# Turning the first 512 rows of x: four row blocks on TensorE, where two were turned on TensorE and two by a transposing load

## The chip, the cores and the metric

The kernel runs on one core of a Trainium2 chip. The metric is the device time of one execution in microseconds (us), as the median of several runs. Engines are named as the profile names them: PE is TensorE's matmul stream and PEld its weight loads, DVE is VectorE, ACT is ScalarE, POOL is GpSimd, SP is the SyncE queue that issues most loads and stores.

## The reference: what is computed

Two independent attention problems, A and B, have the same shape, and their outputs are joined along the last axis. Each has 2048 rows of x with 1024 columns, 32 heads of 32, and a sliding window of 256 keys. In short form:

```python
qkv = (x @ wqkv).reshape(B, S, 3, H, Dh)          # S = 2048, H = 32, Dh = 32
scores = q @ k.T * Dh ** -0.5                     # per head
mask = (i - j >= 0) & (i - j < 256)               # query i, key j
p = softmax(where(mask, scores, -1e9))
out = (p @ v).reshape(B, S, D) @ wo               # D = 1024
result = concatenate([A, B], axis=-1)
```

Inputs and output are bf16.

## The kernel before, in words

**Tiles.** x is held transposed in four quarters of 512 rows per problem, `xT[(pi, k)]`: 128 partitions, eight column tiles (`ct`), 512 rows. A row block is 128 rows, so a quarter has four of them (`QB` = 4). Heads are taken in groups of four (`g`, eight per problem, 16 in all). A group has a weight tile `wqk[g]` with a q half and a k half (`which` 0 and 1), and every two groups share a tile `wv[m]`.

**Chains and sessions.** The TensorE work is of two sorts. Projections are cut into *chains*: eight matmuls of 512 columns, or sixteen of 256, which fill one PSUM bank and end with a cast out of it. There are chains for q and k of a group and a quarter (`qk_steps`, L198), for v of two row blocks (`v_steps`, L216) and for the output (`out_steps`, L262). Their bank comes from `ps_proj`, which has two. A *session* (L438) is the score matmuls of four block pairs (L451), one exp over them on ACT (L459), and the masks on POOL. There are 180 sessions. The PV matmuls with the row sums (L513) follow three sessions after the last scores that they need, then the norm on VectorE.

**What sets the order.** The program is written out in order by a planner. Each chain has an `early` and a `late` session. In each session, `emit` places filler steps from the chain with the smallest `late` that may start, until a budget is spent. The budget is `level(now) - fixed[now]` (L426): the work that must be done by, or is available by, each later session, averaged, and never more than `NS_MOST` = 3300 ns. `fixed` holds 440 ns for a session's scores and 55 ns for each PV step. `forced` (L418) ends what is due. `evacuate` (L188) chooses ScalarE or VectorE for a cast by a model of their clocks (`_Clock`, L60). `whole` says if a chain's matmuls take all 128 output columns at once (L172) or in four strips of 32 (L176); strips are used in sessions in which a PV is due.

**The start, which the change touches.** The kernel begins with dummy matmuls on a zeroed tile, `keep_warm`. Row blocks 0 and 1 of problem A's x are loaded as they lie (L548) into `xrow`, slices of a tile `rows`. `flip(a)` (L575) turns one block: eight 128x128 transposes into one PSUM bank (L578), then a copy of one half of that bank by ACT (L582) and of the other by DVE (L583) into `xT[(0, 0)]`. Row blocks 2 and 3 come by a transposing load, `load_x(0, 0, 2, 2)` (L133, issued on SP). Quarters 1 to 3 come by transposing loads of 512 rows behind it on the same queue, with the weights of group 1 and the second v tile between them. `first(lo, hi)` (L585) does the columns from `lo` to `hi` of q and k of group 0 and quarter 0; q's bank is taken from `ps_acc`, k's from `ps_proj`. `emit(0, chains[0].size)` places one whole v chain; it stands twice, once ahead of the last `first` and once behind it. Then the loop over sessions begins.

Of the kernel before, what the change touches and what calls it, by code (L numbers as in the profile page):

```python
# [8 lines left out]
BF16 = mybir.dt.bfloat16  # L9
F32 = mybir.dt.float32  # L10
# [8 lines left out]
P = 128  # L19
# [7 lines left out]
QB = 4  # L27
SLOTS = 4
# [50 lines left out]
def _fast_path(ctx, tc, cfg, problems, outs, consts, certify):  # L79
    nc = tc.nc  # L80
# [8 lines left out]
    clock = _Clock()  # L89
# [27 lines left out]
    ps_st = ctx.enter_context(tc.tile_pool(name="ps_st", bufs=1, space=PSUM))  # L117
    ps_acc = ctx.enter_context(tc.tile_pool(name="ps_acc", bufs=2, space=PSUM))
    ps_proj = ctx.enter_context(tc.tile_pool(name="ps_proj", bufs=2, space=PSUM))
# [6 lines left out]
    blank = top[:].bitcast(BF16)  # L126

    def new_x(pi, k):
        xT[(pi, k)] = xpool.tile([P, CT, 512], BF16, name="xT")

    def load_x(pi, k, a=0, n=QB, c0=0, c1=CT):
        lo, hi = a * P, (a + n) * P
        nc.sync.dma_start_transpose(  # L133
            out=xT[(pi, k)][:, c0:c1, lo:hi],
            in_=problems[pi][0][k * 512 + lo:k * 512 + hi, c0 * P:c1 * P])
# [7 lines left out]
    def load_wqk(g, which, queue, lo=0, hi=CT):  # L143
        pi, t = divmod(g, T)
        queue.dma_start(out=wqk[g][:, lo:hi, which, :],  # L145
                        in_=wsrc(pi)[:, lo:hi, which, t * P:(t + 1) * P])

    def new_wv(m):
        wv[m] = wvp.tile([P, CT, VG * P], BF16, name="wv")

    def load_wv(m, lo, hi, queue):
        pi, mm = divmod(m, T // VG)
        w_ = VG * P
        queue.dma_start(out=wv[m][:, lo:hi, :],  # L154
                        in_=wsrc(pi)[:, lo:hi, 2, mm * w_:(mm + 1) * w_])
# [9 lines left out]
    def qk_tiles(g):  # L165
        if g not in qks:
            qks[g] = (qkp.tile([P, S], BF16, name="qT"), qkp.tile([P, S], BF16, name="kT"))
        return qks[g]

    def by_columns(out, lo, hi, lhsT, rhs, start, stop):  # L170
        if whole[0]:
            nc.tensor.matmul(out[:, lo:hi], lhsT=lhsT, rhs=rhs, start=start, stop=stop,  # L172
                             skip_group_check=True)
            return
        for c in range(0, P, 32):
            nc.tensor.matmul(out[c:c + 32, lo:hi], lhsT=lhsT[:, c:c + 32], rhs=rhs, start=start,  # L176
                             stop=stop, tile_position=(0, c), skip_group_check=True)
# [4 lines left out]
    def add_or(dst):  # L182
        def f():
            nc.vector.tensor_tensor(out=top[:], in0=top[:], in1=dst.bitcast(I32),
                                    op=ALU.bitwise_or)
        side.append((COST["or"], f, False))

    def evacuate(out, in_, engines=("act", "dve")):  # L188
        if clock.evacuate(engines) == "act":
            nc.scalar.copy(out=out, in_=in_)  # L190
        else:
            nc.vector.tensor_copy(out=out, in_=in_)

    def new_pp():
        clock.chain()
        return ps_proj.tile([P, 512], F32, name="pp")

    def qk_steps(g, which, k, lo=0, hi=512, st_=None, last=True):  # L198
        pi = g // T
        st_ = {} if st_ is None else st_  # L200
        steps = []
        for ct in range(CT):
            def f(ct=ct):
                if "pp" not in st_:
                    st_["pp"] = new_pp()
                by_columns(st_["pp"], lo, hi, wqk[g][:, ct, which, :], xT[(pi, k)][:, ct, lo:hi],
                           ct == 0, ct == CT - 1)
                clock.pe += NS_MM * (hi - lo) / 512.0
                if ct == CT - 1 and last:
                    dst = qk_tiles(g)[which][:, k * 512:(k + 1) * 512]  # L210
                    evacuate(dst, st_["pp"][:])
                    add_or(dst)
            steps.append((NS_MM * (hi - lo) / 512.0, f))
        return steps
# [138 lines left out]
    chains = []  # L353
# [39 lines left out]
    def start_chain(now):  # L393
        for n, c in enumerate(chains):
            if c.early <= now:
                current.extend(chains.pop(n).steps)
                return True
        return False

    def run_side():  # L400
        cost, f, last = side.pop(0)
        f()
        clock.dve = max(clock.dve, clock.pe) + cost
        if last:
            clock.norms.append(clock.dve)

    def emit(now, budget):
        done = 0.0
        while (current or chains) and done < budget - 0.5 * (current[0][0] if current else NS_MM):
            if not current and not start_chain(now):  # L410
                break
            ns, f = current.pop(0)
            f()
            done += ns
            if side and (clock.dve < clock.pe + 100.0 or len(side) > 8):
                run_side()
# [124 lines left out]
    rows = opool.tile([P, T, 512], BF16, name="oT")  # L541
    new_x(0, 0)
    new_wqk(0)
    new_wv(0)
    xrow = [rows[:, 2 * a:2 * a + 2, :].rearrange("p t n -> p (t n)") for a in range(2)]
    load_wqk(0, 0, nc.scalar)
    for a in range(2):
        nc.sync.dma_start(out=xrow[a], in_=problems[0][0][a * P:(a + 1) * P, :])  # L548
        if a == 0:
            load_wqk(0, 1, nc.sync)  # L550
    load_wv(0, 0, CT, nc.sync)
    load_x(0, 0, 2, 2)
    new_x(0, 1)
    load_x(0, 1)
    new_wqk(1)
# [6 lines left out]
            new_wv(1)  # L562
            load_wv(1, 0, CT, nc.sync)

    warm = ps_st.tile([P, 4, SLOTS, P], F32, name="st")[:, 1].rearrange("p a q -> p (a q)")

    def keep_warm(n):
        for _ in range(n):
            nc.tensor.matmul(warm, lhsT=blank[:, 0:P], rhs=blank[:, 0:512], start=True, stop=True)

    keep_warm(6)
    flips = [ps_acc.tile([P, 512], F32, name="acc")[:]]
    held = [{"pp": ps_acc.tile([P, 512], F32, name="acc")[:]}, {}]

    def flip(a):  # L575
        f = flips[0].bitcast(BF16).rearrange("p (ct q) -> p ct q", q=P)
        for ct in range(CT):
            nc.tensor.transpose(out=f[:, ct, :], in_=xrow[a][:, ct * P:(ct + 1) * P],  # L578
                                identity=ident[:])
        dst = xT[(0, 0)][:, :, a * P:(a + 1) * P]  # L580
        half = CT // 2
        nc.scalar.copy(out=dst[:, :half, :], in_=f[:, :half, :])  # L582
        nc.vector.tensor_copy(out=dst[:, half:, :], in_=f[:, half:, :])  # L583

    def first(lo, hi):  # L585
        for which in range(2):
            for _, f in qk_steps(0, which, 0, lo, hi, held[which], last=hi == 512):
                f()

    flip(0)  # L590
    keep_warm(3)
    first(0, P)
    flip(1)
    keep_warm(3)
    first(P, 2 * P)
    emit(0, chains[0].size)
    first(2 * P, 4 * P)
    clock.banks = clock.banks[-2:]
    emit(0, chains[0].size)

    sealed = first_use(G - 1, NQ - 1, 0)
    for now in range(END):
# [3 lines left out]
        while due and due[0][0] <= now:  # L606
            _, pg, pk = due.pop(0)
# [14 lines left out]
    while due:  # L622
        _, pg, pk = due.pop(0)
# [132 lines left out]
def kernel(  # L756
# [48 lines left out]
    with tc.manual_schedule():  # L805
        with ExitStack() as fctx:
            _fast_path(fctx, tc, cfg, problems, outs, consts, [reduce_bits, decide])
# [40 lines left out]
```

## Time and profile before

| | us |
|---|---|
| median of 3 runs | 614.89 (614.78 to 615.02) |
| time of the profiled execution | 614.78 |
| its span in the trace | 613.0 |
| PE busy in the span | 594.8 (97%) |
| ACT busy | 453.7 (74%) |
| DVE busy | 446.8 (73%) |
| POOL busy | 328.0 (54%) |
| mean granted TensorE clock | 0.998 |

The span is the time between the first and the last instruction of the program in the trace; the time of the execution holds 1.8 us more. A busy share is an average over the whole span and tells little of a stage: the change lies in the first 20 us, and is to be read from the timelines of that stretch. In lines of a timeline the first number is the start in us from the span's beginning, the second the length; brackets hold the idle time ahead of the instruction and what ended it. "L172 PE MATMUL pp<-xT,wqk" is a matmul that writes tile pp from xT and wqk, recorded at line 172 of the kernel. Ends of matmuls are modelled, so that neighbouring pieces of PE can overlap.

### The profile page before, as it was taken

What the parts mean: (1) busy time and instruction counts of PE and PEld (TensorE: products, weight loads), DVE (VectorE), ACT (ScalarE), POOL (GpSimd) and SP (SyncE); (2) the same over time, 40 slices, a digit from 0 to 9 for tenths busy, and PEclk for the clock granted to TensorE, in tenths of its full rate; (3) what the DMA queues carried; (4) which work ended last, traced back from release to release, by engine and by line L of the source; (5) the groups of instructions that cost most, each with busy time, mean ns of one, the idle gap of its engine ahead of it and who ended that gap; (6) DMA issues with size and microseconds to landing.
All of it is one profiled execution on the core that took longest, in us unless ns stands there. A gap on an engine that the chain in (4) does not pass through costs nothing.

```text
span 613.0 us, 28647 instructions
## 1 busy us (share of the span) xinstructions
PE 594.8 (97%) x12725; PEld 344.5 (56%) x12777; DVE 446.8 (73%) x1169; ACT 453.7 (74%) x402; POOL 328.0 (54%) x630
## 2 busy tenths in 40 slices
PE   8899999999999999999999999999999999999996
PEld 6455466656655756554555756655445765445443
DVE  1477969887888788769688888877878687779200
ACT  2777888888888878887778777787877777776332
POOL 0465666666666666556565565555555555554000
PEclk9999999999999999999999999999999999999999
DMA  9924110111015601453111100112020030113222
GB/s 209 204 71 106 38 37 4 37 37 40 3 36 89 116 11 31 77 99 80 36 39 37 38 4 3 37 37 81 3 70 30 12 98 19 64 55 113 72 77 65
DMA packets 88594, 35.47 MB, mean 58 GB/s; under 512 B 67600, under 2 KB 88208, under 8 KB 88464
## 3 DMA queue, kind: packets, MB, share of 16 engines
q1 hardware_dynamic: 87424, 33.31, 22.7%
q8 instruction: 102, 1.67, 1.1%
q10 hardware_dynamic: 1040, 0.26, 0.2%
q14 instruction: 28, 0.23, 0.1%
HBM read 17.30 MB, written 8.39 MB: 42 GB/s over the span
## 4 chain that ended last, share of the span: by engine, by line
PE 91%; ACT 3%; issue 2%; DMA 1%; SPq 1%; DVE 0%; ACTq 0%; DVEq 0%
PE pp L176 42%; PE pp L172 26%; PE acc L513 13%; PE st L451 10%; ACT pt L459 2%; DMA xT<-in_A_x_dram 1%; SPq L133 1%; ACT kT L190 0%; ACT vt L190 0%; SPq L548 0%; ACT osb L190 0%; ACT qT L190 0%; DVE rinv L524 0%; SPq L154 0%; SPq L145 0%
## 5 line engine op out<-in xcount | busy, mean ns | idle before, releaser
L459 ACT ACTIVATE pt<-st 128x2048 bf16<-128x2048 f32 x180 | 338.0, 1878 | 87.7 <-PE st L451 67.3
L471 POOL TENSOR_SCALAR_AFFINE_SELECT pt<-pt 128x512 bf16<-128x512 bf16 x224 | 155.3, 693 | 145.5 <-ACT pt L459 144.3
L467 POOL TENSOR_SCALAR_AFFINE_SELECT pt<-pt 128x512 bf16<-128x512 bf16 x256 | 180.0, 705 | 88.3 <-ACT pt L459 88.3
L524 DVE RECIPROCAL rinv<-acc 128x128 f32<-128x128 f32 x128 | 122.1, 954 | 66.7 <-PE acc L513 65.4
L176 PE MATMUL pp<-xT,wqk 128*32 128x512 bf16 x2696 | 162.8, 379 | 0.2
L481 DVE TENSOR_TENSOR both<-pt 128x512 bf16<-128x512 bf16 x224 | 132.5, 631 | 0.0
L176 PEld LDWEIGHTS <-wqk 128*32 128x32 bf16 x2696 | 69.3, 97 | 54.5 <-issue 1.2
L172 PE MATMUL pp<-xT,wqk 128*128 128x512 bf16 (+2 forms) x319 | 75.9, 368 | 6.2 <-issue 3.0
L176 PE MATMUL pp<-wv,xT 128*32 128x256 bf16 x2376 | 74.0, 273 | 0.0
L451 PE MATMUL st<-qT,kT 32*128 32x384 bf16 (+2 forms) x1488 | 71.7, 269 | 0.0
L176 PEld LDWEIGHTS <-xT 128*32 128x32 bf16 x2376 | 62.3, 97 | 5.5
L529 DVE STREAM_SHUFFLE wide<-rinv 128x128 f32<-128x128 f32 x256 | 64.5, 297 | 0.0
L513 PE MATMUL acc<-pt,vt 128*32 128x128 bf16 (+1 forms) x2160 | 63.3, 239 | 0.0
L172 PE MATMUL pp<-wo_sb,oT 128*128 128x512 bf16 (+1 forms) x270 | 59.7, 373 | 1.7 <-issue 1.0
L190 ACT CAST osb<-pp 128x512 bf16<-128x512 f32 (+1 forms) x53 | 30.6, 577 | 39.1 <-PE pp L172 23.1
L451 PEld LDWEIGHTS <-kT 32*128 32x128 bf16 x1488 | 22.3, 92 | 64.3 <-issue 63.4
L531 DVE TENSOR_TENSOR oT<-acc,wide 128x256 bf16<-128x256 f32 x128 | 54.4, 425 | 4.4
L172 PEld LDWEIGHTS <-wqk 128*128 128x128 bf16 x382 | 34.4, 98 | 40.7 <-issue 9.0
L176 PE MATMUL pp<-wo_sb,oT 128*32 128x512 bf16 x948 | 55.4, 379 | 0.7 <-DVE unsafe_i L802 0.7
L172 PE MATMUL pp<-wv,xT 128*128 128x256 bf16 x430 | 53.2, 273 | 2.0 <-ACT kT L190 0.8
L513 PEld LDWEIGHTS <-vt 128*32 128x32 bf16 x2160 | 35.9, 96 | 26.3 <-issue 24.1
L172 PEld LDWEIGHTS <-xT 128*128 128x128 bf16 x430 | 40.6, 98 | 12.8 <-issue 6.0
(45 smaller groups left out, 382.2 us busy)
## 6 DMA issues: line engine op xcount, KB each, us to landing
out_dram<-osb SPq DMA_DIRECT2D x63, 128.0 KB, 1.8
wqk<-in_B_wqkv_dram SPq DMA_DIRECT2D x32, 128.0 KB, 2.7
wqk<-in_A_wqkv_dram SPq DMA_DIRECT2D x24, 128.0 KB, 2.8
wo_sb<-in_A_wo_dram SPq DMA_DIRECT2D x16, 128.0 KB, 2.2
wv<-in_B_wqkv_dram SPq DMA_DIRECT2D x16, 128.0 KB, 2.9
wo_sb<-in_B_wo_dram SPq DMA_DIRECT2D x16, 128.0 KB, 2.4
wv<-in_A_wqkv_dram SPq DMA_DIRECT2D x2, 512.0 KB, 5.7
wv<-in_A_wqkv_dram SPq DMA_DIRECT2D x8, 128.0 KB, 2.3
```

The lines of the kernel that those rows point to most:

```text
L172: nc.tensor.matmul(out[:, lo:hi], lhsT=lhsT, rhs=rhs, start=start, stop=stop, skip_group_check=True)
L176: nc.tensor.matmul(out[c:c + 32, lo:hi], lhsT=lhsT[:, c:c + 32], rhs=rhs, start=start, stop=stop, tile_position=(0, c), skip_group_check=True)
L190: nc.scalar.copy(out=out, in_=in_)
L451: nc.tensor.matmul(st[:, r, a:b, :], lhsT=kT[32 * r:32 * r + 32, j * P:(j + 1) * P], rhs=qT[32 * r:32 * r + 32, q * P:(q + b - a) * P], st ...
L459: nc.scalar.activation(out=pt[:, :, :n, :].rearrange("p r a q -> p r (a q)"), in_=st[:, :, :n, :].rearrange("p r a q -> p r (a q)"), func= ...
L467: nc.gpsimd.affine_select(out=blk, in_=blk, pattern=[[0, 4], [1, P]], compare_op=ALU.is_ge, fill=0.0, base=0, channel_multiplier=-1)
L471: nc.gpsimd.affine_select(out=blk, in_=blk, pattern=[[0, 4], [-1, P]], compare_op=ALU.is_gt, fill=0.0, base=0, channel_multiplier=1)
L481: nc.vector.tensor_tensor(out=both[:, :, h, :], in0=pts[s0][:, :, a0, :], in1=pts[s1][:, :, a1, :], op=ALU.add)
L513: nc.tensor.matmul(acc[32 * r:32 * r + 32, o:o + w_], lhsT=lhsT, rhs=src[:, r, :, :], start=(x == 0), stop=(x == len(moves) - 1), tile_pos ...
L524: nc.vector.reciprocal(out=rinv[:], in_=acc[:, 2 * P:3 * P])
L529: nc.vector.stream_shuffle(out=wide[:, h * P:(h + 1) * P], in_=rinv[:], mask=[16 * h] * 32)
L531: nc.vector.tensor_tensor(out=oTs[(pi, k)][:, t, (p % 2) * 256:(p % 2 + 1) * 256], in0=acc[:, 0:256], in1=wide[:], op=ALU.mult)
```

## The change

All four row blocks of the first quarter are loaded as they lie and turned with `flip`, and the transposing load of the last two goes. The two added loads stand on SP ahead of the load of `wv[0]`; row block 1 now stands ahead of the k half of `wqk[0]`. The banks change: the warm tile comes from `ps_proj`; flips 0, 1 and 3 use tiles of `ps_acc` and flip 2 one bank of the score tile; q and k of group 0 take both their banks from `ps_proj`. `first(which, lo)` now does 256 columns of one of q and k. The order becomes flip 0, flip 1, q of rows 0 to 255, flips 2 and 3, k of rows 0 to 255, q and k of rows 256 to 511. One v chain is placed ahead of the first session, where two were. The warm matmuls after flip 0 become four. The planner's functions and constants are the same in both.

```diff
-    xrow = [rows[:, 2 * a:2 * a + 2, :].rearrange("p t n -> p (t n)") for a in range(2)]
+    xrow = [rows[:, 2 * a:2 * a + 2, :].rearrange("p t n -> p (t n)") for a in range(QB)]
     load_wqk(0, 0, nc.scalar)
-    for a in range(2):
+    for a in range(QB):
         nc.sync.dma_start(out=xrow[a], in_=problems[0][0][a * P:(a + 1) * P, :])
-        if a == 0:
+        if a == 1:
             load_wqk(0, 1, nc.sync)
     load_wv(0, 0, CT, nc.sync)
-    load_x(0, 0, 2, 2)
     new_x(0, 1)
     load_x(0, 1)
...
-    warm = ps_st.tile([P, 4, SLOTS, P], F32, name="st")[:, 1].rearrange("p a q -> p (a q)")
+    warm = ps_proj.tile([P, 512], F32, name="pp")
...
     keep_warm(6)
-    flips = [ps_acc.tile([P, 512], F32, name="acc")[:]]
-    held = [{"pp": ps_acc.tile([P, 512], F32, name="acc")[:]}, {}]
+    flips = [ps_acc.tile([P, 512], F32, name="acc") for _ in range(2)]
+    flips = [f[:] for f in flips]
+    flips.append(ps_st.tile([P, 4, SLOTS, P], F32, name="st")[:, 0].rearrange("p a q -> p (a q)"))
+    flips.append(None)
+    held = [{}, {}]
 
     def flip(a):
-        f = flips[0].bitcast(BF16).rearrange("p (ct q) -> p ct q", q=P)
+        if a == 3:
+            flips[a] = ps_acc.tile([P, 512], F32, name="acc")[:]
+        f = flips[a].bitcast(BF16).rearrange("p (ct q) -> p ct q", q=P)
...
-    def first(lo, hi):
-        for which in range(2):
-            for _, f in qk_steps(0, which, 0, lo, hi, held[which], last=hi == 512):
-                f()
+    def first(which, lo):
+        for _, f in qk_steps(0, which, 0, lo, lo + 256, held[which], last=lo > 0):
+            f()
 
     flip(0)
-    keep_warm(3)
-    first(0, P)
+    keep_warm(4)
     flip(1)
     keep_warm(3)
-    first(P, 2 * P)
-    emit(0, chains[0].size)
-    first(2 * P, 4 * P)
-    clock.banks = clock.banks[-2:]
+    first(0, 0)
+    flip(2)
+    flip(3)
+    first(1, 0)
+    first(0, 256)
+    first(1, 256)
     emit(0, chains[0].size)
```

More of the change, by code (lines that the diff above doesn't have):

```diff
@@ L563, in _fast_path @@
             load_wv(1, 0, CT, nc.sync)
-    warm = ps_st.tile([P, 4, SLOTS, P], F32, name="st")[:, 1].rearrange("p a q -> p (a q)")
+    warm = ps_proj.tile([P, 512], F32, name="pp")
     def keep_warm(n):
         for _ in range(n):
-            nc.tensor.matmul(warm, lhsT=blank[:, 0:P], rhs=blank[:, 0:512], start=True, stop=True)
+            nc.tensor.matmul(warm[:], lhsT=blank[:, 0:P], rhs=blank[:, 0:512], start=True, stop=True)
     keep_warm(6)
-    flips = [ps_acc.tile([P, 512], F32, name="acc")[:]]
-    held = [{"pp": ps_acc.tile([P, 512], F32, name="acc")[:]}, {}]
+    flips = [ps_acc.tile([P, 512], F32, name="acc") for _ in range(2)]
[3 more added lines that the diff above has]
+    held = [{}, {}]
     def flip(a):
-        f = flips[0].bitcast(BF16).rearrange("p (ct q) -> p ct q", q=P)
+        if a == 3:
+            flips[a] = ps_acc.tile([P, 512], F32, name="acc")[:]
+        f = flips[a].bitcast(BF16).rearrange("p (ct q) -> p ct q", q=P)
         for ct in range(CT):
```

## The prediction

> **What bounds the kernel now.** I read the page's chain of waits first. It runs through TensorE for 91% of the span, so a change counts only by what it does to TensorE's clock time.
>
> ```profile
> PE 91%; ACT 3%; issue 2%; DMA 1%; SPq 1%; DVE 0%; ACTq 0%; DVEq 0%
> ```
>
> The same chain in order of time, cut to the first 60 us, has one stretch that is not TensorE: until 17.1 us the chain is SP's queue and one DMA.
>
> ```profile
> 2.82 5.92 SPq L133
> ...
> 8.79 8.28 DMA xT<-in_A_x_dram
> ...
> 17.11 0.39 PE pp L172
> ```
>
> L133 is the transposing load. The first piece is the issue of the half-size load that the change removes; behind it stands the load of the second x quarter, which lands at 8.79 + 8.28 = 17.07. The timeline of SP gives the order of the issues (start, length):
>
> ```profile
> 0.80 0.40 SPq L548 DMA_DIRECT2D oT<-in_A_x_dram  x1
> 1.25 0.42 SPq L145 DMA_DIRECT2D wqk<-in_A_wqkv_dram  x1
> 1.73 0.57 SPq L548 DMA_DIRECT2D oT<-in_A_x_dram  x1
> 2.34 0.43 SPq L154 DMA_DIRECT2D wv<-in_A_wqkv_dram  x1
> 2.82 10.57 SPq L133 DMA_TRANSPOSE xT<-in_A_x_dram  x2
> ```
>
> The timeline of TensorE shows what it does meanwhile:
>
> ```profile
> 4.33 1.04 PE L578 MATMUL acc<-ident,oT 128*128 128x128 bf16 x8 [0.28 <-DMA oT<-in_A_x_dram]
> 5.16 1.49 PE L569 MATMUL st<-top 128*128 128x512 bf16 x3
> ...
> 7.43 0.61 PE L578 MATMUL acc<-ident,oT 128*128 128x128 bf16 x8
> 7.88 0.81 PE L569 MATMUL st<-top 128*128 128x512 bf16 x3
> 8.72 0.84 PE L172 MATMUL acc<-xT,wqk 128*128 128x128 bf16 x8
> ...
> 9.84 1.91 PE L172 MATMUL pp<-wv,xT 128*128 128x256 bf16 x16
> 11.77 1.03 PE L172 MATMUL acc<-xT,wqk 128*128 128x256 bf16 x8
> 12.64 1.04 PE L172 MATMUL pp<-xT,wqk 128*128 128x256 bf16 x8
> 13.52 1.91 PE L172 MATMUL pp<-wv,xT 128*128 128x256 bf16 x16
> 15.36 0.40 PE L451 MATMUL st<-qT,kT 32*128 32x384 bf16 x8
> 17.11 1.25 PE L172 MATMUL pp<-xT,wqk 128*128 128x512 bf16 x4 [1.36 <-DMA xT<-in_A_x_dram]
> ```
>
> Ends are modelled and overlap; I use start to start. All other work of the start is done by 15.72, and TensorE then stands 1.36 us until 17.07. That is the longest idle stretch of TensorE between its first useful matmul and its last. The copies out of a turned block, from the timelines of ScalarE and VectorE:
>
> ```profile
> 8.08 0.59 ACT L582 COPY xT<-acc 128x512 bf16<-128x512 bf16 x1 [2.08 <-PE acc L578]
> 8.70 0.42 DVE L583 COPY xT<-acc 128x512 bf16<-128x512 bf16 x1 [2.25 <-ACT xT L582]
> ```
>
> They run one after the other (8.67, then 8.70). The projection's first four steps need only ScalarE's half, so they start at 8.72.
>
> **What the skill says.** The Trainium skill, "PSUM — Partial Sum Buffer", section "PSUM bank collisions raise a hardware error", says that two engines must not touch one bank at once, ScalarE against VectorE included. The trace agrees: 0.03 us between the two copies of one bank, never an overlap. Copies of two flips in two banks may overlap. "TensorE: Matmul & The Clock Gate", section "What's actually happening", gives a warm-up of about 3.4 us of activity; the trace has cold 512-column matmuls 0.43 us apart (six in 2.74), and three in 0.81 us at 7.88. Both kernels fill TensorE alike until about 6 us, so I give both the same warm-up. "DMA: Bandwidth & Descriptors", section "Issuing engines are not separate DMA queues", says that loads of all queues share the same engines; the landings here do queue up behind one another.
>
> **Part by part, up to the point where x's second quarter is first used.** I call that point X. At X both kernels have done block 0's q and k, the v chains of rows 0 to 3 and session 0. X is 17.11 before.
>
> *Loads.* The half-size transposing load (5.92 us of SP's queue) goes; two row loads come (0.40 to 0.57 each). The first transposing load is issued at about 2.82 + 2 x 0.5 = 3.85 rather than 8.79. By the trace's issue-to-landing times (7.9 to 9.1 us, queue included) it lands at 12 to 13. An upper bound: wv's 512 KB now has 512 KB more ahead of it; wv alone landed at 2.34 + 6.7 = 9.04, and 512 KB there took 9.04 - 7.33 = 1.7, so wv lands at 10.8 and x 5 us after it at worst, 15.8. The later loads are issued some 4 us sooner; nothing waits for them before either. Landings before: row block 0 at 0.80 + 3.5 = 4.3, wqk's q half (ACT queue) at 5.5, its k half at 6.65, row block 1 at 7.33. Row block 1 moves ahead of the k half: 6.65 at the latest. Then the k half at 7.3, row block 2 at about 8.2, row block 3 at 9.04, where the same 1.5 MB had landed before.
>
> *TensorE.* Flip 0 and its copies do not move. Four warm matmuls from 5.16: the fourth, warm by then, ends at about 6.5 (6.9 if cold). Flip 1 starts at 6.6. ScalarE's copy is done 1.29 later as before (7.43 to 8.72), so `first(0, 0)` starts at 7.9; three warm matmuls cover the gap. Eight 256-column matmuls take 0.87 (11.77 to 12.64): 8.77. Flips 2 and 3 take 0.45 each (7.43 to 7.88): 9.22, 9.67. `first(1, 0)`: 10.54. Meanwhile flip 2's copy starts on ScalarE at 8.77 + 0.65 = 9.42 and ends at 10.01; flip 3's on ScalarE from 10.03 to 10.62; VectorE's half of flip 3 ends at 11.07. So `first(0, 256)` starts at 10.67, a wait of 0.13, and its second four steps at 11.11 find VectorE done. 11.54; `first(1, 256)` 12.41. The v chain takes 1.93 (9.84 to 11.77); its bank, q's, is free at 11.74 + 0.59 = 12.33. 14.3. Session 0 takes 0.36: 14.7. The second v chain is no longer placed ahead of it; with `late` = 1 it is the first chain that session 0's filler takes, 1.9 more: X = 16.6.
>
> As differences: two flips +0.9; four groups of 128 columns (7.43 - 6.44 and 9.84 - 8.72, 2.1) become two of 256 (1.74), -0.4; the fourth warm matmul +0.16; the copy wait +0.13; the second v chain's 1.9 for 1.84, +0.06; the DMA stall -1.36. Together -0.5.
>
> What the trace of before cannot show: row block 3 has 0.2 of slack; landing 0.5 late costs 0.3. Flip 1 starts 0.4 late if the fourth warm matmul is cold. Landings that are early gain at most 0.3, since the copies bind next. X moves by -0.8 to +0.2; I take -0.5.
>
> *Order of sessions.* 1728 planned ns of filler move from ahead of session 0 to behind it. The planner's level is then set by all work that is available before session 85: 2827 ns before, worked out from its lists, against a distance of 2.83 us between sessions in the trace. With 1728 more it is 2848: sessions 1 to 85 each carry 0.02 more, session 1 starts some 1.5 us sooner, and by session 85 (261 us) both kernels have done the same work. No TensorE work is made by that, except that in sessions with PV the projections go in four column strips: 40 of them take 2.33 us, ten whole ones about 2.17. For some 1 us of work moved there, +0.1.
>
> *Cover.* The four extra copies (two of 0.59, two of 0.42) lie on ScalarE and VectorE while both were idle: 3.1 us on ScalarE before 11.79. Flip 2 in the score tile's bank must be copied before session 0: 10.5 against 14.3.
>
> **Sum.** Profiled execution: span 613.0, time 614.78, so 1.8 around it. 614.78 - 0.5 + 0.1 = 614.4; the median of the runs, 614.89, stands 0.1 above: 614.5. A measurement of this kernel can tell about 0.2%, 1.2 us, from no change, so this is no change.
>
> **Rivals.**
>
> *Slower, at 616.3.* The new phase between chains and sessions makes TensorE wait for evacuations. From the waits of TensorE (total, times, longest):
>
> ```profile
> PE pp L172 <- ACT vt L190: 1.2, 3, 0.5
> PE pp L172 <- ACT kT L190: 1.2, 3, 0.4
> ```
>
> A cast that ScalarE gets just after an exp starts up to 1.9 us late; the next chain needs its bank and TensorE stands 0.4 to 0.5. Up to session 85 every chain now ends up to 1728 planned ns further on, against other exps, and the planner, which knows neither the DMA stall of before nor its absence, may choose other engines for casts. For: such waits exist before, with both engines busy for 7 to 8 tenths of a slice. Against: those of ScalarE's casts are seven, 2.8 us in the whole span, four of them (1.6 us) before session 85, and a new draw of the same lottery has no direction. It decides from four more such waits (4 x 0.45 = 1.8) than before: 614.5 + 1.8 = 616.3.
>
> *Faster, at 613.2.* X moves by the full -0.8 and the four early waits mostly fall away, for 1.0 more: 614.78 - 0.8 - 1.0 + 0.1 + 0.1 = 613.2. For: nothing obliges the waits to return. Against: it needs both.
>
> *The stall stays.* The transposing load could be no sooner, if its 8.3 us are not the queue ahead of it but the engines themselves: then TensorE stands from 16.6 to 17.1, X does not move, and the time is 615.0. For: the first such load was 5.92 us in the issue alone. Against: it would have to land more than 13 us after its issue, where the longest took 9.1. It lies within no change.
>
> **How the numbers follow.** The forecast, with the stall that stays, 0.60; four more waits or worse 0.26; the faster case 0.14. More is given to waits than to their absence because the start after the change has no idle stretch left that hides a late row block: every 0.1 that it is late adds to the waits. The likeliest case alone runs from 613.7 to 615.7: 615.0 with X unmoved, X's bounds of -0.8 to +0.2, and one wait (0.45) more or less. The range for 8 in 10 takes in the faster case and, on the other side, one wait more than the slower rival's four (616.3 + 0.45): 613.2 to 616.8. No change 0.60, slower 0.26, faster 0.14.
>
> **What would show it.** Right: no wait of TensorE for xT's DMA; the first transposing load issued at about 3.9 and landed before 16; four flips with their copies, the last ended by about 11.1; session 0's scores at 14.3, one microsecond sooner than the 15.36 of before; the first matmul of x's second quarter at 16.6; sessions 1 to 8 still 2.8 apart, session 85 at 261 within 1 us. Wrong: a wait on row blocks 2 or 3 ahead of the flips, a cold TensorE after 7 us, a landing of x's second quarter after 16.6, or a list of TensorE's waits for casts that has grown by over 1.2 us with X where I put it.

## The result, and the profile after

| | before | changed |
|---|---|---|
| median, us (runs) | 614.95 (6) | 613.23 (6) |
| lowest to highest | 614.44 to 615.23 | 612.66 to 613.67 |
| ratio, 95% interval | | 0.9972 [0.9959, 0.9985] |
| profiled execution, span | 614.78, 613.0 | 613.21, 611.5 |

The change is faster by 0.28%, 1.7 us. In two later groups of runs the ratio was 0.9975 [0.9967, 0.9984] and 0.9974 [0.9964, 0.9983]. That is inside the stated range by 0.03 us, and the median of the third group, 613.10, lies below it: that the range held is in part luck. No change, the likeliest case, did not come, and the faster case did.

The chain of waits in order of time, changed kernel, cut to 30 us (start, length, what):

```profile
0.80 0.40 SPq L548
1.20 0.06 issue
1.25 4.83 DMA oT<-in_A_x_dram
6.09 0.05 issue
6.13 0.62 PE acc L582 x8
6.75 0.65 PE pp L568 x3
7.40 0.03 issue
7.43 1.06 PE pp L172 x8
```

From 6.13 on the chain is TensorE. What is left of DMA in it is the landing of row block 1 at 1.25 + 4.83 = 6.08; the transposing load is gone from the chain. SP's queue, changed kernel (start, length of the issue):

```profile
0.80 0.87 SPq L548 DMA_DIRECT2D oT<-in_A_x_dram  x2
1.73 0.43 SPq L145 DMA_DIRECT2D wqk<-in_A_wqkv_dram  x1
2.19 1.05 SPq L548 DMA_DIRECT2D oT<-in_A_x_dram  x2
3.29 0.43 SPq L154 DMA_DIRECT2D wv<-in_A_wqkv_dram  x1
3.77 7.95 SPq L133 DMA_TRANSPOSE xT<-in_A_x_dram  x1
```

The second quarter's load begins at 3.77 instead of 8.79 and lands 10.0 us later, at 13.8. The timeline of TensorE, changed kernel:

```profile
4.26 0.94 PE L582 MATMUL acc<-ident,oT 128*128 128x128 bf16 x8 [0.21 <-DMA oT<-in_A_x_dram]
5.03 1.03 PE L568 MATMUL pp<-top 128*128 128x512 bf16 x4
6.13 0.62 PE L582 MATMUL acc<-ident,oT 128*128 128x128 bf16 x8
6.59 0.81 PE L568 MATMUL pp<-top 128*128 128x512 bf16 x3
7.43 1.06 PE L172 MATMUL pp<-xT,wqk 128*128 128x256 bf16 x8
8.32 0.61 PE L582 MATMUL st<-ident,oT 128*128 128x128 bf16 x8
8.77 0.61 PE L582 MATMUL acc<-ident,oT 128*128 128x128 bf16 x8
9.21 2.81 PE L172 MATMUL pp<-xT,wqk 128*128 128x256 bf16 x24
11.86 1.91 PE L172 MATMUL pp<-wv,xT 128*128 128x256 bf16 x16
13.70 0.40 PE L451 MATMUL st<-qT,kT 32*128 32x384 bf16 x8
14.03 1.92 PE L172 MATMUL pp<-wv,xT 128*128 128x256 bf16 x16
15.79 0.81 PE L172 MATMUL pp<-xT,wqk 128*128 128x512 bf16 x2
```

No line from 6.13 on has idle time ahead of it. X, the first matmul of the second quarter, is at 15.79; it was 17.11. The copies behind flips 2 and 3 on ScalarE, then on VectorE:

```profile
8.97 0.59 ACT L586 COPY xT<-st 128x512 bf16<-128x512 bf16 x1 [1.59 <-PE st L582]
9.45 0.59 ACT L586 COPY xT<-acc 128x512 bf16<-128x512 bf16 x1
...
9.59 0.42 DVE L587 COPY xT<-st 128x512 bf16<-128x512 bf16 x1 [1.75 <-ACT xT L586]
10.07 0.42 DVE L587 COPY xT<-acc 128x512 bf16<-128x512 bf16 x1
```

Here VectorE copies from one bank (9.59 to 10.01) while ScalarE copies from the other (9.45 to 10.04). ScalarE's are done at 10.04, when k's columns 0 to 255 are (9.21 + 0.87 = 10.08), and VectorE's at 10.49, ahead of the second four steps of the next projection (10.08 + 0.44 = 10.52). TensorE shows no wait for them.

Between X and session 85 the change gains as well. The starts of the sessions, changed less before, are -1.86 at session 28 and -1.61 at session 85; X alone is -1.32. The waits of TensorE between X and session 85 (total, times, longest), before and then changed:

```profile
PE pp L172 <- ACT vt L190: 0.8, 2, 0.5
PE pp L172 <- ACT qT L190: 0.4, 1, 0.4
PE pp L172 <- ACT kT L190: 0.4, 1, 0.4
```

```profile
PE pp L172 <- ACT kT L190: 0.6, 2, 0.4
PE pp L172 <- ACT qT L190: 0.4, 1, 0.4
PE pp L176 <- ACT kT L190: 0.4, 1, 0.4
PE pp L172 <- ACT vt L190: 0.3, 1, 0.3
```

One of the two waits for a v cast is gone: the one of session 13, here in the timeline of TensorE before.

```profile
56.64 0.59 PE L172 MATMUL pp<-xT,wqk 128*128 128x512 bf16 x2 [0.51 <-ACT vt L190]
```

Nor does a matmul come 0.24 late any more that does so in before at 85.72, too short a delay for the lists; and a wait of 0.19 for k's cast has come at 74.3. Together that is the 0.54 that is gained from X to session 28. In session 60 a wait of 0.12, which the list of before leaves out, has grown to 0.40 (from 189.8 on) and shows as +0.28 at the next session. So the listed waits alone add up to nearly the same in both, 1.6 and 1.7. The order of sessions, too, is in the result. The question for the runs was how much is X and how much is order.

### The profile page after: what moved, and what is told of

It reads as the page before. It is cut to its first block, busy times and chain, and to the rows that moved or that the text cites. A ratio compares the mean times of both kernels' runs of the same rounds, so it can differ in the third digit from the quotient of the medians.

```text
span 611.5 us, 28734 instructions
## 1 busy us (share of the span) xinstructions
PE 594.7 (97%) x12765; PEld 344.6 (56%) x12817; DVE 447.4 (73%) x1171; ACT 454.5 (74%) x404; POOL 329.3 (54%) x630
## 4 chain that ended last, share of the span: by engine, by line
PE 93%; ACT 3%; issue 1%; DMA 1%; DVE 1%; SPq 0%; ACTq 0%; DVEq 0%
PE pp L176 42%; PE pp L172 28%; PE acc L513 13%; PE st L451 10%; ACT pt L459 2%; DMA oT<-in_A_x_dram 1%; ACT kT L190 0%; DVE rinv L524 0%; PE acc L582 0%; ACT vt L190 0%; ACT osb L190 0%; DVE top L184 0%; DVE qT L192 0%; DVE both L481 0%; PE pp L568 0%
## 5 line engine op out<-in xcount | busy, mean ns | idle before, releaser
L172 PE MATMUL pp<-xT,wqk 128*128 128x512 bf16 (+1 forms) x326 | 77.5, 369 | 4.3 <-issue 2.9
L176 PEld LDWEIGHTS <-xT 128*32 128x32 bf16 x2424 | 63.6, 97 | 5.8
L172 PE MATMUL pp<-wv,xT 128*128 128x256 bf16 x418 | 51.5, 273 | 2.0 <-ACT kT L190 1.0
L172 PEld LDWEIGHTS <-xT 128*128 128x128 bf16 x418 | 39.2, 98 | 13.0 <-issue 6.9
```

## The experiments

**The first group** asked that: the changed kernel again; before with one v chain ahead of session 0; the changed kernel with two; and the changed kernel with its load held back.

*The changed kernel again.* No edit.

> The changed kernel once more, as the anchor for the others of this group and for a second record of the start. All theories: about 613.2 us, 0.997 of before. Theory of the stall (the gain is the 1.36 us for which TensorE stood for the second x quarter, and the start is now bound by TensorE itself): X, the first matmul of the second quarter, at 15.8 again within 0.3, no wait on xT's DMA. Theory of the warm-up (the gain is that TensorE was warm at 5.1 us in this one record and cold until 6.4 in the other): in another record the four warm matmuls after flip 0 may be cold, 0.43 apart, and X at 16.2 or later.

Measured: 613.61, 0.9975 [0.9967, 0.9984]. Timeline of TensorE:

```profile
5.08 1.91 PE L568 MATMUL pp<-top 128*128 128x512 bf16 x4
6.79 0.75 PE L582 MATMUL acc<-ident,oT 128*128 128x128 bf16 x8
...
16.57 0.81 PE L172 MATMUL pp<-xT,wqk 128*128 128x512 bf16 x3
```

The same four warm matmuls take 1.71 to the next start, 0.43 each; in the first record they took 1.10. Flip 1 is 0.66 later and X at 16.57 rather than 15.79. So X moves between executions of one program by 0.8, with TensorE's warm-up, and the first record was an early one. The gain in the median is nevertheless the same. From X to session 85 the sessions move by the same -0.29 against before as in the first record: that part repeats from one execution to the next.

*One chain ahead, in the kernel before.*

```diff
     first(2 * P, 4 * P)
     clock.banks = clock.banks[-2:]
-    emit(0, chains[0].size)
```

> The kernel before, with one v chain ahead of session 0 where it has two, as the change has; loads, flips and projections as before. Theory of the stall: session 0 comes 1.8 us sooner, the second v chain follows it, and TensorE then stands for the second quarter as before; X stays at 17.1 and the time at 614.6 to 615.0. Theory of the new draw (the gain comes from where chains fall against exps once one chain is moved behind session 0): the sessions fall as in the changed kernel and the time goes to about 613.3.

Measured: 614.44, 0.9993 [0.9984, 1.0001]. TensorE:

```profile
17.20 0.82 PE L172 MATMUL pp<-xT,wqk 128*128 128x512 bf16 x3 [0.50 <-DMA xT<-in_A_x_dram]
```

X stays, at 17.20, and the wait on the load is there: 0.50, with another 0.68 in front of session 0, which now follows k's cast at once. The time goes down by 0.5 at the most likely, and the interval just reaches no change. So order alone gives some, and not the whole: the theory of the new draw falls as the only cause. Session 85 stands at -0.41 where X stands at +0.09, so -0.50 lies between; the wait of session 60 is 0.12 here, as in before. Counted from X, its sessions 1 to 60 lie within 0.07 of those of the changed kernel, and the last session within 0.02. So these two kernels have one order and differ, but for single waits, in X alone. What lies between their medians, 614.44 and 613.61, is what the start is worth: 0.8, or 1.1 by the two ratios (0.9993 and 0.9975).

*Two chains ahead, in the changed kernel.*

```diff
     first(1, 256)
     emit(0, chains[0].size)
+    emit(0, chains[0].size)
```

> The changed kernel with both v chains ahead of session 0, as before had them. Theory of the stall: X stays at 15.8, session 0 comes 1.8 us later, the time is 613.2 to 613.6 (the waits for casts between session 1 and 30 were 0.2 to 0.3 us less in the changed kernel and may come back). Theory of the new draw: back to 614.6 to 615.0.

Measured: 613.80, 0.9985 [0.9979, 0.9992], between the changed kernel and before. The first matmul of the second quarter, which here has the same work ahead of it, is at 16.25, in a record where the four warm matmuls took 1.57. The wait for a v cast in session 13 is back:

```profile
55.78 0.81 PE L172 MATMUL pp<-xT,wqk 128*128 128x512 bf16 x3 [0.51 <-ACT vt L190]
```

Counted from X, sessions 1 to 62 lie within 0.04 of those of before: the order is before's again. By the ratios it is worth some 0.6 of the 1.5 (0.9985 against 0.9975), by the medians 0.2 (613.80 against 613.61), and the two intervals overlap; the start is the rest.

*The load held back.*

```diff
     new_x(0, 1)
+    new_x(0, 2)
+    load_x(0, 2, 2, 2)
     load_x(0, 1)
...
     for k in range(2, NQ):
-        new_x(0, k)
+        if k > 2:
+            new_x(0, k)
         load_x(0, k)
```

> The changed kernel with a transposing load of 256 rows still issued ahead of that of the second quarter; its data go to the place of the third quarter, which is loaded again later, and are not used. Theory of the stall: the issue of the second quarter's load starts some 5 us later, at about 9, it lands at 17 to 19 (8 to 10 us from its issue), TensorE stands 1.3 to 3 us at X, and the time is 614.5 to 616.2, at or above before, though four flips are made on TensorE. Theories of the new draw and of the warm-up: no change from 613.2, since TensorE's program is the same.

Measured: 616.90, 1.0025 [1.0017, 1.0033], slower than before. TensorE, and its busy time and clock in stretches of the same record (stretch, length, PE, PEld, DVE, ACT, POOL busy, granted clock, DMA share, GB/s):

```profile
18.44 1.31 PE L172 MATMUL pp<-xT,wqk 128*128 128x512 bf16 x3 [2.13 <-DMA xT<-in_A_x_dram]
```

```profile
16.30:18.40 2.10, 0.01 (x1) 0.00 (x0) 0.69 (x1) 0.23 (x1) 1.80 (x3) 1.00 1.02 225
18.40:20.00 1.60, 1.56 (x11) 0.40 (x11) 0.00 (x0) 0.00 (x0) 0.00 (x1) 0.57 0.88 126
20.00:22.00 2.00, 2.00 (x13) 0.67 (x6) 0.00 (x0) 1.65 (x1) 0.00 (x0) 0.50 1.28 290
22.00:24.00 2.00, 2.00 (x17) 0.76 (x16) 1.36 (x2) 0.23 (x1) 1.22 (x2) 0.99 0.92 209
```

TensorE's instructions are those of the changed kernel; only the load is late. That alone takes the whole gain and 1.5 more. The stall is 2.13 and X is 18.44. Behind it the granted clock is 0.5 for some 3.5 us: session 1 follows X after 1.25 instead of 0.74, and session 2 follows session 1 after 3.90 instead of 2.81, another 1.6. The expectation had the stall and not the clock; the time is 0.7 above its range. So it is that load that decides: with a 256-row transposing load ahead of it the start is bound by its landing, whoever turns the row blocks. The kept load adds its own 512 KB (256 rows of 1024 in bf16) to its place in the queue, and no run parts the two.

**The second group** asked which side binds the start, and tried two versions.

*More warm matmuls, in the changed kernel (first edit) and in the one before (second edit), after flip 0.*

```diff
-    keep_warm(4)
+    keep_warm(8)
```

```diff
     flip(0)
-    keep_warm(3)
+    keep_warm(7)
     first(0, P)
```

> The changed kernel with eight warm matmuls after flip 0 where it has four. Theory that the start of the changed kernel is bound by TensorE: the four more take 0.22 each, warm by then even in a record that begins cold, so X goes from 15.8 to 16.6 to 16.6 to 17.4 and the time up by 0.6 to 0.9, to about 614.3. Theory that some transfer still binds it: no change from 613.5.

> The kernel before with seven warm matmuls after flip 0 where it has three. Theory that the start of the kernel before is bound by the landing of the second x quarter at 17.1: the four more (0.9 to 1.7) only shorten the stall of 1.36, X stays at 17.1 to 17.4 and the time within 0.3 of before. Theory that TensorE's own work bound it: up by 0.9 or more.

Measured: 614.02, 0.9993 [0.9985, 1.0001] for the first, where the changed kernel stands at 0.9975: some 1.1 us of the time. (In this group the version with two warm matmuls, below, has 612.90: 1.1 less as well.) 614.51, 1.0002 [0.9994, 1.0010] for the second: nothing. That is the clearest difference between the two starts: TensorE's own work counts in one and is hidden in the other. In the record of the first, X is 16.04, sooner than expected and inside the changed kernel's own scatter; only the medians carry the point. In the record of the second, session 0 is 0.75 later than in before, the load lands 0.4 sooner (8.79 + 7.9 = 16.7), and the wait for it has shrunk:

```profile
16.72 2.55 PE L172 MATMUL pp<-xT,wqk 128*128 128x512 bf16 x11 [0.22 <-DMA xT<-in_A_x_dram]
```

*Rows ahead of weights.*

```diff
-    load_wqk(0, 0, nc.scalar)
     for a in range(QB):
-        nc.sync.dma_start(out=xrow[a], in_=problems[0][0][a * P:(a + 1) * P, :])
-        if a == 1:
-            load_wqk(0, 1, nc.sync)
+        queue = nc.scalar if a == 1 else nc.sync
+        queue.dma_start(out=xrow[a], in_=problems[0][0][a * P:(a + 1) * P, :])
+        if a == 0:
+            load_wqk(0, 0, nc.sync)
+    load_wqk(0, 1, nc.sync)
...
     flip(0)
-    keep_warm(4)
     flip(1)
-    keep_warm(3)
+    keep_warm(2)
+    flip(2)
     first(0, 0)
-    flip(2)
     flip(3)
```

> The changed kernel with the four row blocks loaded ahead of both halves of the weights except q's (row block 1 on ACT's queue), flip 1 straight behind flip 0, two warm matmuls, then flip 2 ahead of the first projection, so that it fills the time of the copies. Theory that TensorE's start binds: X sooner by 0.6 to 1.2, at 14.6 to 15.6, if the second quarter's load, issued at 3.8 as before, lands by 13.8 again; time 612.2 to 612.9. If the row blocks' landings bind instead: TensorE waits ahead of flips 0 and 1 and X gains nothing.

Measured: 613.16, 0.9980 [0.9973, 0.9988], no better than the changed kernel. Two row blocks in flight at once land at 4.9 and 4.6 (0.80 + 4.1 and 0.80 + 3.8), the first of them later than alone (4.2 in the change): TensorE waits 0.93 for flip 0, which starts at 4.99. The v load's issue now takes 1.43 and the second quarter's begins at 4.78; it lands 10.5 later, at 15.3, and X at 15.34 waits 0.1 for it. X is the soonest of all, but the time is above the 612.2 to 612.9 that were expected with it.

*Two warm matmuls.*

```diff
-    keep_warm(4)
+    keep_warm(2)
```

> The changed kernel with two warm matmuls after flip 0 where it has four. In the record with a warm TensorE the four ended 0.1 before row block 1 landed (6.1); in the one with a cold TensorE they ended at 6.8 and flip 1 was 0.66 late. With two, flip 1 starts at 6.1 to 6.2 either way, so X lies at 15.8 to 16.1 and the time at 613.0 to 613.4, with less spread than the changed kernel, unless the lost activity keeps TensorE cold for longer: then flips and the first projection take up to twice as long, and X goes to 16.6 or later.

Measured: 612.90, 0.9975 [0.9965, 0.9984], X at 15.38, flip 1 at 5.74.

**The third group** put the changed kernel, the kernel before and two versions on one chip.

> The changed kernel once more, beside the two versions of this group, so that they are compared on one chip. 0.9975 of before; X at 15.8 where TensorE is warm by the warm matmuls after flip 0, up to 16.6 where it is not.

> The kernel before once more, for a second record of its start. Theory that its start is bound by the landing of the second x quarter: X within 0.3 of 17.1 and again a wait on xT's DMA, however warm TensorE is.

> The version with two warm matmuls after flip 0 once more, beside the changed kernel. If four cold warm matmuls are what delays flip 1 in the slower runs of the changed kernel: 612.9, some 0.4 to 0.6 below the changed kernel in the median, X at 15.4 to 15.8, and again little spread. If the first time was the chip: equal to the changed kernel.

Measured: changed 613.10, 0.9974 [0.9964, 0.9983], X at 16.67, with the four warm matmuls 0.43 apart again. Before 614.58, 1.0001 [0.9993, 1.0010], and here the expectation missed: X at 16.29.

```profile
16.29 2.55 PE L172 MATMUL pp<-xT,wqk 128*128 128x512 bf16 x10 [0.62 <-DMA xT<-in_A_x_dram]
```

The wait is there, but the load, issued at 8.46 and 7.8 on its way, lands 0.8 sooner than in the first record: the landing of before scatters as the warm-up of the changed kernel does. Two warm matmuls: 613.17, 0.9982 [0.9976, 0.9989]. Its record has X at 15.52 and 612.47, the lowest of the profiled executions, but its median is that of the changed kernel. What one record of each seemed to promise, the runs do not show.

*q's weights third.*

```diff
-    load_wqk(0, 0, nc.scalar)
     for a in range(QB):
         nc.sync.dma_start(out=xrow[a], in_=problems[0][0][a * P:(a + 1) * P, :])
         if a == 1:
-            load_wqk(0, 1, nc.sync)
+            load_wqk(0, 0, nc.sync)
+    load_wqk(0, 1, nc.sync)
...
-    keep_warm(4)
+    keep_warm(1)
```

> The changed kernel with all loads of the start on SP in the order row blocks 0 and 1, q's weights, row blocks 2 and 3, k's weights, v's weights, and one warm matmul after flip 0. If landings set when flip 1 can start: row block 1 lands at 4.7 to 5.2 rather than 5.7 to 6.1, the first projection starts at 6.1 to 6.6 rather than 7.0 to 7.4, X at 14.5 to 15.2 and the time at 612.0 to 612.6, if the second quarter, issued at 4.3, lands by 14.3. If the second quarter binds again, as in the version with rows first where it landed 10.5 us after its issue: X at 14.8 with a wait on xT's DMA.

Measured: 613.30, 0.9979 [0.9971, 0.9988]. The first projection starts at 6.31, 1.1 sooner than in the first record of the change, and it is given back: 0.40 for k's weights, and at X

```profile
16.17 0.82 PE L172 MATMUL pp<-xT,wqk 128*128 128x512 bf16 x2 [0.62 <-DMA xT<-in_A_x_dram]
```

The second quarter, issued at 5.44, lands 10.7 later; X at 14.8 was expected for that case. No version beats the change clearly.

**All records together.** The profiled execution's time less its X is what comes after X. Without the held-back load:

| order | kernel: X, time, difference |
|---|---|
| two v chains ahead | before 17.11, 614.78, 597.67; again 16.29, 614.20, 597.91; more warm matmuls 16.72, 614.62, 597.90; changed with two chains 16.25, 614.55, 598.30 |
| one v chain ahead | changed 15.79, 613.21, 597.42; again 16.57, 613.62, 597.05; again 16.67, 613.70, 597.03; before with one chain 17.20, 614.55, 597.35; more warm matmuls 16.04, 613.04, 597.00; rows first 15.34, 612.92, 597.58; two warm 15.38, 612.92, 597.54; again 15.52, 612.47, 596.95; q third 16.17, 613.34, 597.17 |

The two groups do not overlap: 597.95 in the mean of four, 597.23 in the mean of nine, 0.7 less with one chain. X is 16.70 in the two records of before and 16.34 in the three of the change, 0.4 less.

Not all of the 0.7 is order. The starts of three sessions in the timelines, counted from each record's X and less those of before's first record:

| | session 60 | session 85 | session 179, the last |
|---|---|---|---|
| before, again | -0.03 | -0.03 | +0.11 |
| changed, two chains ahead | -0.02 | +0.42 | +0.93 |
| before, one chain ahead | -0.50 | -0.50 | -0.50 |
| changed, each of three records | -0.57 | -0.29 | -0.52 or -0.53 |

Up to session 60 the order alone parts the kernels, whichever start they have. The +0.93 of the record with two chains is lost in sessions 64, 100 and 158, and the largest piece, 0.44 in session 64, is in no other record. What follows the last session differs by up to 0.6 between records, and by 0.5 among the three of the change. So 0.5 is what the records show of the order.

## Why the prediction came out as it did

**The load.** Right. Issued at 3.77 for the 3.85 forecast; no wait for it at X; landed at 13.8 for 12 to 13, with 15.8 as the upper bound. The duration that I took, 7.9 to 9.1 from issue to landing, was too short: with more plain loads ahead in the queue it is 10.0. The rival that the stall stays is refuted by the trace. Of the other landings, row block 3, which the sum had only 0.2 ahead of its flip, was not waited for; row block 1 was what flip 1 waited for in the first record (6.08, then 6.13), 0.5 sooner than the sum had it start.

**TensorE's steps.** From flip 1 on, forecast and first record, in distances: to `first(0, 0)` 1.3 and 1.30; that projection 0.87 and 0.89; the flips 0.45 each and 0.45, 0.44; the three further projections and the copy wait 2.74 and 2.65; v 1.9 and 1.84; session 0 0.36 and 0.33; second v 1.9 and 1.76. The copy wait of 0.13 did not appear. That is 0.3 less in all.

**The warm-up.** I gave both kernels the same one, and took the fourth warm matmul alone as warm. In the first record all four were warm, in the two others all four cold, as the six of the beginning. That is the 0.47 by which flip 1 was sooner than forecast in the first record, and the 0.2 by which it was later in the others. X, forecast at 16.6, came at 15.79, 16.57 and 16.67; the forecast of -0.5 is near the difference of the means, -0.4, but two and three records that scatter by 0.8 cannot size it, and the runs put the start at 0.8 to 1.1. I gave X of before no scatter, and it was 17.11 and 16.29. Which term of X was too small in the runs without a profile stays open.

**The order of sessions** is the step that failed. The prediction put it at +0.1, for work moved into sessions with strips, and left the waits for casts to a lottery without direction. The records show -0.3 to session 85 and -0.5 to the last, in all three of the change, and the runs 0.2 to 0.6. The price of the strips was not the fault: up to session 60, 13 more matmuls go in strips, 12 of them of v, for less than the 0.1 that I gave. The lottery of waits is drawn once, when the instructions are written out, and then repeats in each execution, but for single waits: that of session 60 did not grow in the version with q's weights third, though TensorE's order is the same there. The wait of 0.5 in session 13 could have been read as one that hangs on the phase: in before's timeline the last matmul of a v chain starts at 54.12, 0.33 into that session, and the exp that its cast has to wait for at 54.24. The prediction also spread the head start of session 1 over 85 sessions. Counted from X it was 1.75 at session 1 and was used up, but for 0.54, at session 28.

**The sum.** In the runs the start is worth 0.8 to 1.1 and the order 0.4 to 0.5 (before with two chains ahead and with one, 614.93 and 614.44; ratio 0.9993); together that is the 1.3 to 1.7 of the medians, where the prediction had -0.5 and +0.1. The records alone show less: X -0.4 and all that follows -0.7 make -1.1. The profiled executions of the change lie 0.2 above their medians on average, those of before some 0.3 below, so the rest is of the size of what a record differs from its median. How X is spread over the executions without a profile, no run here shows. Nor does one part what the start is made of on TensorE: two flips more, coarser projections and other banks came together.

**The rivals.** The slower one named the right mechanism, casts behind exps, with the wrong sign. The faster one asked for X at -0.8 and four waits mostly gone. In the median the start gave 0.8 to 1.1 and the order 0.4 to 0.5, with no four waits gone. The 0.14 that I gave it for needing both at once was too little: each showed without the other, in before with one chain ahead and in the changed kernel with two.

## What to carry to other kernels

When the chain of waits at the start is a queue, look at what stands ahead of the load that ends it. Here taking one load out of the queue was worth more than the work that it added to TensorE, up to where TensorE itself bound the start. Test which side binds by adding known work to each: what is hidden in one kernel and counts in the other names the bound. And where a planner writes the order out, a changed start changes every phase behind it. Most of those waits repeat in each execution, so undo the order alone before the start gets the credit, and do not take the size of a term from one or two profiles.

## What the runs showed of the hardware that was not expected

TensorE's warm-up is not the same in each execution of one program. The four matmuls from 5.0 to 5.1 us took 1.10, 1.57, 1.71 and 1.71 to the next start in four records with the same instructions up to there.

In the one record with a stall of 2.13 us the granted clock went to 0.5 behind it, for some 3.5 us; behind the stalls of 1.36 in before and 0.62 in its second record it stayed at 1.00. The Trainium skill, "TensorE: Matmul & The Clock Gate", section "What's actually happening", speaks of an idle window of about 3.4 us with boundaries that run freely; here less than that was idle, and the measurement decides. The runs of that kernel lie from 614.78 to 617.38, so it may not happen in each.

A transposing load of 512 rows took 7.6 to 10.7 us from issue to landing, and its issue alone held SP for 4.1 to 8.0 us; both were longest for the second quarter where it stands behind row and weight loads (10.0 and 7.95 in the change). The plain load behind it in the queue was issued only when that was over (11.77 in the change, after 3.77 + 7.95 = 11.72). Where the plain loads ahead took longer to issue, it came later (4.78 with rows first, 5.44 with q's weights third). Its position in SP's queue was the whole question in the versions that tried to start sooner.
